# A gated recurrence and a mixture of experts in fp32: the recurrence on two sequences at a time, with matmuls that alternate between halves of the array

## The chip, the cores and the metric

One core of a Trainium2 chip. The metric is the device time of one execution in microseconds: 672.98 us for the kernel before, the median of three runs (672.84 to 673.34).

## The reference

Two parts in a row, all in fp32. The first is a recurrence per batch b and head h (4 x 8 of them, 768 steps, head size 48) whose state, a 48x48 matrix, decays by a gate f per row and step:

```python
f = 1.0 / (1.0 + np.exp(-f_logit))
for t in range(S):
    state = f[:, :, t, :, None] * state + np.einsum('bhd,bhe->bhde', k[:, :, t], v[:, :, t])
    y[:, :, t] = np.einsum('bhd,bhde->bhe', q[:, :, t], state)
```

Its 3072 x 384 output x goes into the second part: each token takes the best of 4 groups (logits `x @ w_group`), in it the best of 4 experts (`x @ w_expert[g]`), and gets `gate * relu(x @ w1) @ w2` of that one expert (w1 384x1024, w2 1024x384).

## The kernel before, in words

**The recurrence** (L111 to L248) works on chunks of 128 tokens of one sequence, `order` = chunk by chunk and within it sequence by sequence, 24 chunks in all. A chunk goes through five stages, functions of the kernel, and in step i of a loop the five stages run on five chunks, the oldest first:

- `gated` (L131): loads f, q, k and v (192 KB each, SP queue); exp and ln on ScalarE (ACT) make -log f; a matmul with `cum` (tile cs) sums it from the chunk's middle; transposes (nt) and a reduction give the chunk's whole decay; exp of the sums, times q and k, gives qh (VectorE, DVE) and kh (GpSimd, POOL).
- `turned` (L166): transposes qh and kh, so that heads lie on partitions, two heads a on the two halves of 64 (rows 0 to 47 and 64 to 111): tiles Tq and Tk.
- `scored` (L176): ap = k q^T for each head (48 rows of the array, 128 columns), first the four heads of the lower half of partitions, then those of the upper; DVE masks it with `tri` into am.
- `weighed` (L187): y = am v (128 rows, 48 columns) and sp q (48 rows, 48 columns; sp is the scaled state), first one half, then the other; ACT copies y to xT. ds = kh v updates the state st.
- `done` (L219): gate logits lg = gw xT (20 x 128, stationary gw) into logitsT, transposes back to tokens (x_ps), DVE copies x, SP stores it to x_dram.

A matmul in fp32 is two passes on TensorE (PE) in the trace, each with its own weight load; a transpose is one. Tiles of PSUM come from one pool of 8 banks in rotation. Tile, the scheduling layer, puts each engine's instructions in an order of its own, and the engine follows that in order.

**The join**: when all chunks are done, a flag `fari` (the largest sum of -log f against a bound) is read by every engine, and a branch skips the slow exact scan. **The routing** (L317 to L437) starts with 24 transposes of logitsT (tile logits, L343) and is a chain on DVE after that. **The experts** (L440 on): 16 experts, 256 slots each, weights three deep in the pool `wp`; the weights of the first experts are loaded in the recurrence already.

Of the kernel before, what the change touches and what calls it, by code (L numbers as in the profile page):

```python
# [1 line left out]

# [6 lines left out]
FP32 = mybir.dt.float32  # L9
# [6 lines left out]
P = 128  # L16
# [3 lines left out]
def kernel(  # L20
# [38 lines left out]
    wp = ctx.enter_context(tc.tile_pool(name="wp", bufs=3))  # L59
# [14 lines left out]
    tri = const([P, P], FP32, "tri")            # 1 where row <= column  # L74
    strict = const([P, P], FP32, "strict")      # 1 where row < column
    cum = const([P, P], FP32, "cum")            # sums from the chunk's middle
# [10 lines left out]
    nc.vector.tensor_scalar(cum, tri, halves[:, 0:1], None, OP.subtract)  # L87
# [5 lines left out]
    # gate weights with the rows in the order of xT: a head to each 64 partitions  # L93
    gw = const([P, HP, NL], FP32, "gw")
    nc.vector.memset(gw, 0.0)
    for r in range(2):
        rows = slice(DP * r, DP * r + D)
        nc.sync.dma_start(out=gw[rows, :, 0:G], in_=moe_w_group.rearrange("(a r d) g -> r d a g", r=2, d=D)[r])
        for g in range(G):
            nc.sync.dma_start(out=gw[rows, :, G + g * EG:G + (g + 1) * EG], in_=moe_w_expert[g].rearrange("(a r d) e -> r d a e", r=2, d=D)[r])  # L100

    logitsT = const([NL, N], FP32, "logitsT")
    sums = const([P, NT, HP, 2], FP32, "sums")

    def chunk_logits(n, xT):
        lg = bank([NL, P], "lg")
        for a in range(HP):
            nc.tensor.matmul(lg, lhsT=gw[:, a, :], rhs=xT[:, a, :], start=(a == 0), stop=(a == HP - 1))  # L108
        nc.vector.tensor_copy(logitsT[:, n * P:(n + 1) * P], lg)  # L109

# [1 line left out]
    with ExitStack() as fast:  # L112
        sb = fast.enter_context(tc.tile_pool(name="sb", bufs=3))
        NROT = 5
        pads = {}
        for nm in ("nl", "qh", "kh"):
            pads[nm] = [const([P, H, DP], FP32, f"{nm}{i}") for i in range(NROT)]
            for t in pads[nm]:
                nc.vector.memset(t[:, :, D:DP], 0.0)
        NX = 3  # L120
        xTs = [const([P, HP, P], FP32, f"xT{i}") for i in range(NX)]
        for t in xTs:
            nc.vector.memset(t, 0.0)
        state = {}

        order = [(b, c) for c in range(NC) for b in range(B)]
        live = {}

        def gated(i):
            """Loads, decay sums, and the gated q and k with heads on partitions."""  # L130
            b, c = order[i]  # L131
            n = b * NC + c
            ld = {}
            for nm, src in (("f", f_logit), ("q", q), ("k", k), ("v", v)):
                ld[nm] = sb.tile([P, H, D], FP32, tag="ld_" + nm, bufs=5, name="ld_" + nm)
                nc.sync.dma_start(out=ld[nm], in_=src[b, :, c * P:(c + 1) * P, :].rearrange("h t d -> t h d"))
            nl, qh, kh = (pads[nm][i % NROT] for nm in ("nl", "qh", "kh"))

            # -log f = ln(1 + exp(-f_logit)); a value below -44 is over SAFE and sets the scan going
            ex = sb.tile([P, H, D], FP32, tag="ex", name="ex")  # L140
            nc.vector.tensor_scalar(ex, ld["f"], -44.0, None, OP.max)
            nc.scalar.activation(ex, ex, AF.Exp, bias=0.0, scale=-1.0)
            nc.scalar.activation(nl[:, :, 0:D], ex, AF.Ln, bias=1.0, scale=1.0)  # L143

            cs = bank([P, DM], "cs")
            nc.tensor.matmul(cs.rearrange("t (h d) -> t h d", d=D), lhsT=cum, rhs=nl[:, :, 0:D], start=True, stop=True)  # L146
            nt = bank([P, HP, P], "nt")
            nlp = nl.rearrange("t (a r) d -> t a (r d)", r=2)
            for a in range(HP):
                nc.tensor.transpose(out=nt[:, a, :], in_=nlp[:, a, :], identity=ident)  # L150
            # the bounds are met by every sum below SAFE; they keep what the scan replaces finite
            mid = sb.tile([P, DM], FP32, tag="mid", name="mid")
            nc.vector.tensor_scalar(mid, cs, SAFE, -SAFE, OP.min, OP.max)
            nc.vector.reduce_sum(out=sums[:, n], in_=nt.rearrange("p a (e t) -> p a e t", e=2), axis=AX)
            gl = sb.tile([P, HP, 2], FP32, tag="gl", bufs=4, name="gl")
            nc.scalar.activation(gl, sums[:, n], AF.Exp, bias=0.0, scale=-1.0)
            eq = sb.tile([P, DM], FP32, tag="eq", name="eq")
            ek = sb.tile([P, DM], FP32, tag="ek", name="ek")
            nc.scalar.activation(ek, mid, AF.Exp, bias=0.0, scale=1.0)  # L159
            nc.scalar.activation(eq, mid, AF.Exp, bias=0.0, scale=-1.0)  # L160
            nc.gpsimd.tensor_tensor(kh[:, :, 0:D], ld["k"], ek.rearrange("t (h d) -> t h d", d=D), OP.mult)  # L161
            nc.vector.tensor_tensor(qh[:, :, 0:D], ld["q"], eq.rearrange("t (h d) -> t h d", d=D), OP.mult)
            live[i] = {"v": ld["v"], "qh": qh, "kh": kh, "gl": gl}

        def turned(i):
            w = live[i]  # L166
            for nm in ("q", "k"):
                pt = bank([P, HP, P], "tr_" + nm)
                tp = w[nm + "h"].rearrange("t (a r) d -> t a (r d)", r=2)
                for a in range(HP):  # L170
                    nc.tensor.transpose(out=pt[:, a, :], in_=tp[:, a, :], identity=ident)
                w[nm] = sb.tile([P, HP, P], FP32, tag="T" + nm, name="T" + nm)
                (nc.vector.tensor_copy if nm == "q" else nc.scalar.copy)(w[nm], pt)

        def scored(i):
            w = live[i]  # L176
            w["am"] = []
            for r in range(2):
                rows = slice(DP * r, DP * r + D)
                ap = bank([P, HP, P], "ap")  # L180
                for a in range(HP):
                    nc.tensor.matmul(ap[:, a, :], lhsT=w["k"][rows, a, :], rhs=w["q"][rows, a, :], start=True, stop=True)  # L182
                t = sb.tile([P, HP, P], FP32, tag=f"am{r}", bufs=2, name=f"am{r}")
                nc.vector.tensor_tensor(t, ap, tri.unsqueeze(1).broadcast_to((P, HP, P)), OP.mult)  # L184
                w["am"].append(t)

        def weighed(i):  # L187
            """The chunk's outputs, and the state that it leaves."""
            b, c = order[i]
            w = live[i]  # L190
            gl = w["gl"]
            if c:
                sp = sb.tile([P, HP, D], FP32, tag="sp", name="sp")
                nc.vector.tensor_tensor(sp, state[b], gl[:, :, 0:1].broadcast_to((P, HP, D)), OP.mult)
            w["xT"] = xT = xTs[i % NX]
            for r in range(2):
                rows = slice(DP * r, DP * r + D)
                y = bank([P, HP, P], "y")
                for a in range(HP):
                    nc.tensor.matmul(y[rows, a, :], lhsT=w["v"][:, 2 * a + r, :], rhs=w["am"][r][:, a, :], start=(a == 0), stop=(c == 0), skip_group_check=True)  # L200
                if c:
                    for a in range(HP):
                        nc.tensor.matmul(y[rows, a, :], lhsT=sp[rows, a, :], rhs=w["q"][rows, a, :], start=False, stop=True, skip_group_check=True)  # L203
                nc.scalar.copy(xT[rows], y[rows])  # L204

            if c < NC - 1:
                ds = bank([P, HP, D], "ds")
                for a in range(HP):
                    for r in range(2):
                        nc.tensor.matmul(ds[DP * r:DP * r + DP, a, :], lhsT=w["kh"][:, 2 * a + r, :], rhs=w["v"][:, 2 * a + r, :], start=True, stop=True)  # L210
# [317 lines left out]
```

## Time and profile before

| what | before |
|---|---|
| median of the runs | 672.98 us |
| the profiled execution: span of its instructions | 672.1 us |
| of this: recurrence, to the last x_ps on PE | 0 to 246.0 us |
| flag, branch, routing, to the first expert matmul | 246.0 to 298.8 us |
| experts | 298.8 to 672.1 us |
| PE busy | 604.9 us (90%) |
| DVE, ACT, POOL busy | 240.6, 116.0, 89.8 us |

The profiled execution is known by its span; the runs' median is 0.9 us above that, for what lies around the span. A timeline row has the start, the duration of the whole group, engine, line, operation, tiles, and shapes; "48*128 48x128" is 48 rows and 128 columns of the array with 48x128 moving elements. PE is pipelined, so a pass is longer (some 0.27 us) than the step from one pass to the next: time per stage is read from the start of one group to the start of the next. The granted clock printed for the first 28 us is not to be trusted; durations tell it there.

### The profile page before, as it was taken

The numbers are of one execution on the slowest core, as the hardware profiler recorded it, in microseconds if no ns is written. First come the engines' busy times: TensorE is split into PE (matmuls) and PEld (weight loads), VectorE is DVE, ScalarE is ACT, GpSimd is POOL, SyncE is SP. The second block draws the span as 40 slices with busy tenths as digits, with TensorE's granted clock in tenths as the row PEclk, the third lists the DMA queues.
The fourth block names the chain that finished last, engine by engine and source line by source line (L and its number), as shares of the span: only waits on it lengthen the run. The fifth ranks groups of instructions, "written<-read, shape, count | busy, mean of one in ns | idle before, by whom it ended". The sixth has DMA issues, their size and how long they took to land. (4 is left out here: it accounts for less than half of the span.)

```text
span 672.1 us, 8713 instructions
## 1 busy us (share of the span) xinstructions
PE 604.9 (90%) x3485; PEld 461.8 (69%) x3485; DVE 240.6 (36%) x548; ACT 116.0 (17%) x258; POOL 89.8 (13%) x104
## 2 busy tenths in 40 slices
PE   4999999999999963569999999999999999999993
PEld 2788888888888842447766776677667767776772
DVE  4586557556555426931111111111111211121110
ACT  3454444333322210000000000000000000000000
POOL 1111011011001000040121122012201220111001
PEclk9999999999999996559999999999999999999998
DMA  6577666858660000023463646264635453540000
GB/s 122 115 150 158 130 131 142 212 155 241 152 205 27 24 27 1 0 81 108 135 228 109 213 138 223 109 217 140 207 127 203 149 195 139 185 140 17 13 7 19
DMA packets 132562, 85.62 MB, mean 127 GB/s; under 512 B 104208, under 2 KB 123701, under 8 KB 132514
## 3 DMA queue, kind: packets, MB, share of 16 engines
q1 hardware_dynamic: 128418, 73.97, 38.7%
q0 software_dynamic: 4096, 11.02, 4.6%
q8 instruction: 30, 0.49, 0.3%
q14 instruction: 18, 0.15, 0.1%
HBM read 75.53 MB, written 11.01 MB: 129 GB/s over the span
## 5 line engine op out<-in xcount | busy, mean ns | idle before, releaser
L461 PE MATMUL hp<-xe,w 128*128 128x256 f32 x768 | 173.1, 386 | 15.4 <-DVE xe L456 15.4
L461 PEld LDWEIGHTS hp<-xe,w 128*128 128x128 f32 x768 | 146.7, 193 | 39.3 <-DVE xe L456 19.4
L469 PE MATMUL yo<-w,h 128*128 128x384 f32 x512 | 167.7, 486 | 0.0
L469 PEld LDWEIGHTS yo<-w,h 128*128 128x128 f32 x512 | 97.3, 190 | 64.4
L465 ACT ACTIVATE h<-hp 128x256 f32<-128x256 f32 x64 | 24.5, 383 | 368.3 <-PE hp L461 324.0
L463 DVE TENSOR_SCALAR h<-hp 128x256 f32<-128x256 f32 x64 | 27.2, 424 | 154.2 <-PE hp L461 112.0
L471 DVE TENSOR_SCALAR yt<-yo,slots 128x384 f32<-128x384 f32 x32 | 19.8, 618 | 148.5 <-PE yo L469 148.5
L472 POOL DMA_INDIRECT out_dram<-yt,slot_tok x32 | 32.3, 1010 | 256.1 <-DVE yt L471 248.3
L161 POOL TENSOR_TENSOR kh<-ld_k,ek 128x384 f32<-128x384 f32 x24 | 24.1, 1003 | 198.2 <-ACT ek L159 129.7
L200 PE MATMUL y<-am,ld_v 128*48 128x128 f32 x384 | 50.5, 283 | 0.0
L200 PEld LDWEIGHTS y<-am,ld_v 128*48 128x48 f32 x384 | 39.0, 126 | 8.0 <-DVE logitsT L109 3.9
L444 POOL DMA_INDIRECT xg<-x_dram,slot_tok x32 | 31.2, 974 | 90.8 <-PE xg_ps L455 45.7
L203 PE MATMUL y<-Tq,sp 48*48 48x128 f32 x320 | 42.8, 274 | 0.0
L182 PE MATMUL ap<-Tq,Tk 48*128 48x128 f32 x384 | 42.4, 291 | 0.0
L182 PEld LDWEIGHTS ap<-Tq,Tk 48*128 48x128 f32 x384 | 37.7, 193 | 2.0 <-issue 0.6
L204 ACT COPY xT<-y 48x512 f32<-48x512 f32 x48 | 27.7, 577 | 64.7 <-PE y L203 61.2
L184 DVE TENSOR_TENSOR am<-ap,tri 128x512 f32<-128x512 f32 x48 | 31.2, 686 | 20.7 <-PE ap L182 20.7
L203 PEld LDWEIGHTS y<-Tq,sp 48*48 48x48 f32 x320 | 32.6, 119 | 7.4 <-issue 7.4
L146 PE MATMUL cs<-nl,cum 128*128 128x384 f32 x48 | 22.0, 542 | 9.6 <-ACT nl L143 9.6
L428 PE MATMUL table<-val,lane 128*128 128x108 f32 x48 | 15.3, 486 | 11.7 <-DVE val L427 11.7
L108 PE MATMUL lg<-xT,gw 128*20 128x128 f32 x192 | 25.2, 274 | 0.7 <-ACT xT L204 0.7
L428 PEld LDWEIGHTS table<-val,lane 128*128 128x128 f32 x48 | 12.1, 313 | 15.9 <-DVE val L427 12.9
(123 smaller groups left out, 453.7 us busy)
## 6 DMA issues: line engine op xcount, KB each, us to landing
w<-in_moe_w_dram SPq DMA_DIRECT2D x32, 1536.0 KB, 7.2
ld_f<-in_f_logit_dram SPq DMA_DIRECT2D x24, 192.0 KB, 3.7
ld_q<-in_q_dram SPq DMA_DIRECT2D x24, 192.0 KB, 3.7
ld_k<-in_k_dram SPq DMA_DIRECT2D x24, 192.0 KB, 3.7
ld_v<-in_v_dram SPq DMA_DIRECT2D x24, 192.0 KB, 3.0
x_dram<-x SPq DMA_DIRECT2D x24, 192.0 KB, 2.0
xg<-x_dram,slot_tok POOLq DMA_INDIRECT x32, 5.1
out_dram<-yt,slot_tok POOLq DMA_INDIRECT x32, 2.6
```

The source lines that it names most:

```text
L108: nc.tensor.matmul(lg, lhsT=gw[:, a, :], rhs=xT[:, a, :], start=(a == 0), stop=(a == HP - 1))
L182: nc.tensor.matmul(ap[:, a, :], lhsT=w["k"][rows, a, :], rhs=w["q"][rows, a, :], start=True, stop=True)
L184: nc.vector.tensor_tensor(t, ap, tri.unsqueeze(1).broadcast_to((P, HP, P)), OP.mult)
L200: nc.tensor.matmul(y[rows, a, :], lhsT=w["v"][:, 2 * a + r, :], rhs=w["am"][r][:, a, :], start=(a == 0), stop=(c == 0), skip_group_check=True)
L203: nc.tensor.matmul(y[rows, a, :], lhsT=sp[rows, a, :], rhs=w["q"][rows, a, :], start=False, stop=True, skip_group_check=True)
L204: nc.scalar.copy(xT[rows], y[rows])
L428: nc.tensor.matmul(table.rearrange("p b t -> p (b t)"), lhsT=lane, rhs=val.rearrange("p b t -> p (b t)"), start=(n == 0), stop=(n == NT - 1))
L444: nc.gpsimd.indirect_dma_start(out=t, out_offset=None, in_=x_dram[:, :], in_offset=bass.IndirectOffsetOnAxis(ap=rows, axis=0))
L461: nc.tensor.matmul(hp, lhsT=w1[:, ko, fo * P:(fo + 1) * P], rhs=xt[:, ko, :], start=(ko == 0), stop=(ko == KO - 1))
L463: nc.vector.tensor_scalar(h[:, fo, :], hp, 0.0, None, OP.max)
L469: nc.tensor.matmul(yp, lhsT=h[:, fo, j * P:(j + 1) * P], rhs=w2[:, fo, :], start=(fo == 0), stop=(fo == FO - 1))
L472: nc.gpsimd.indirect_dma_start(out=out, out_offset=bass.IndirectOffsetOnAxis(ap=rows[j], axis=0), in_=y, in_offset=None, bounds_check=N - ...
```

## The change

The unit of work is now one chunk of two sequences (12 units, pairs s of sequences), and the loop has 16 steps in place of 28. What is computed of the reference is the same.

- All tiles of `gated` have a dimension for the two sequences: 384 KB loads, 768 elements per partition for ACT, DVE and POOL. The sums run from the chunk's start (`tri` in place of `cum`), so the clamp `mid`, the reduction `sums` and the transposes nt are gone; the chunk's whole decay g is the last column of transposes of eq (gt). eq is made by ACT straight from PSUM. qh moves from DVE to POOL, kh from POOL to DVE, the copy Tq from DVE to ACT.
- `scored` alternates lower and upper half of the rows matmul by matmul, into two banks. `weighed` puts the two sequences on the two halves of the columns: y from the state uses all four quarters in turn, y from am the two column halves. `done` has the two sequences on two row halves, and the logits' matmul is turned round: xT is the stationary side (48 rows x 128 columns), gw the moving one (20 columns), so logits come out with tokens on partitions (lgall) and the routing's 24 transposes go.
- The stages are generators, cut where a bank is finished, and a table (WEAVE) sets how they are interleaved in one step.
- The loads of gw move from the SP queue to the ACT queue. Recurrence pools have two buffers; the third pair of expert weights has a pool of its own (wq), which takes the room that the recurrence leaves, so it is loaded after the branch.

The core of the diff:

```diff
-        order = [(b, c) for c in range(NC) for b in range(B)]
+        units = [(c, s) for c in range(NC) for s in range(B // 2)]
...
+    lgall = const([P, NT, NL], FP32, "lgall")
...
-        nc.sync.dma_start(out=gw[rows, :, 0:G], in_=moe_w_group.rearrange("(a r d) g -> r d a g", r=2, d=D)[r])
+        nc.scalar.dma_start(out=gw[rows, :, 0:G], in_=moe_w_group.rearrange("(h d) g -> d h g", d=D))
...
+            for b in range(2):
+                cs = bank([P, H, D], "cs")
+                nc.tensor.matmul(cs.rearrange("t h d -> t (h d)"), lhsT=tri, rhs=nl[:, b], start=True, stop=True)
+                nc.scalar.activation(eq[:, b, :, 0:D], cs, AF.Exp, bias=0.0, scale=-1.0)
+                nc.scalar.activation(ek[:, b], cs, AF.Exp, bias=0.0, scale=1.0)
+                yield
+            nc.gpsimd.tensor_tensor(heads(qh)[:, :, 0:D], heads(w["q"]), heads(eq)[:, :, 0:D], OP.mult)
+
+            nc.vector.scalar_tensor_tensor(out=heads(kh)[:, :, 0:D], in0=heads(ek), scalar=math.exp(SAFE), in1=heads(w["k"]), op0=OP.min, op1=OP.mult)
...
         def scored(i):
             w = live[i]
...
-            for r in range(2):
-                rows = slice(DP * r, DP * r + D)
-                ap = bank([P, HP, P], "ap")
-                for a in range(HP):
-                    nc.tensor.matmul(ap[:, a, :], lhsT=w["k"][rows, a, :], rhs=w["q"][rows, a, :], start=True, stop=True)
+            for b in range(2):
+                ap = [bank([P, HP, P], f"ap{r}") for r in range(2)]
                 for a in range(HP):
                     for r in range(2):
+                        rows = slice(DP * r, DP * r + D)
+                        nc.tensor.matmul(ap[r][:, a, :], lhsT=w["Tk"][rows, b, a, :], rhs=w["Tq"][rows, b, a, :], start=True, stop=True)
+                for r in range(2):
+                    nc.vector.tensor_tensor(w["am"][:, b, r], ap[r], tri.unsqueeze(1).broadcast_to((P, HP, P)), OP.mult)
+                yield
...
+            if c:
+                for a in range(HP):
+                    for r in range(2):
+                        rows = slice(DP * r, DP * r + D)
+                        for b in range(2):
+                            nc.tensor.matmul(ys[r][DP * b:DP * b + DP, a, :], lhsT=old[rows, b, a, :], rhs=w["Tq"][rows, b, a, :], start=(a == 0), stop=False, skip_group_check=True)
+            yield
+            for a in range(HP):
+                for r in range(2):
+                    for b in range(2):
+                        nc.tensor.matmul(ys[r][DP * b:DP * b + DP, a, :], lhsT=w["v"][:, b, 2 * a + r, :], rhs=w["am"][:, b, r, a, :], start=(c == 0 and a == 0), stop=True, skip_group_check=True)
...
+            lg = [bank([P, NL], f"lg{b}") for b in range(2)]
+            for h in range(H):
+                for b in range(2):
+                    rows = slice(DP * b, DP * b + D)
+                    nc.tensor.matmul(lg[b], lhsT=xT[rows, h % 2, h // 2, :], rhs=gw[rows, h, :], start=(h == 0), stop=(h == H - 1))
...
+        WEAVE = (("s", 1), ("t", 1), ("d", 1), ("s", 1), ("t", 1), ("d", 1), ("g", 1), ("w", 2), ("t", 1), ("w", 1), ("g", 1), ("t", 1), ("g", 1), ("d", 1), ("t", 1), ("g", 1))
...
-        logits = bank([P, NT, NL], "logits")
-        for n in range(NT):
-            nc.tensor.transpose(out=logits[:, n, :], in_=logitsT[:, n * P:(n + 1) * P], identity=ident[0:NL, 0:NL])
-        L = logits.rearrange("p n (a e) -> p n a e", e=4)
+        L = lgall.rearrange("p n (a e) -> p n a e", e=4)
```

How the instructions stand. On PE, before, one step of the loop in the middle of the recurrence (each row's last number is how often it repeats):

```order
L200 MATMUL y<-am_1546,ld_v 48x128 x4
L203 MATMUL y<-Tq,sp 48x128 x4
L200 MATMUL y<-am_1553,ld_v 48x128 x4
L203 MATMUL y<-Tq,sp 48x128 x4
L210 MATMUL ds<-ld_v,kh_134 64x48 x8
L182 MATMUL ap<-Tq,Tk 128x128 x8
L171 MATMUL tr_q<-ident,qh_121 128x128 x4
L171 MATMUL tr_k<-ident,kh_131 128x128 x4
L146 MATMUL cs<-nl_112,cum 128x384
L150 MATMUL nt<-ident,nl_112 128x128 x4
L108 MATMUL lg<-xT_142,gw 20x128 x4
L227 MATMUL x_ps<-ident,xT_142 128x128 x4
```

Each stage is one piece, and each half of the array has its piece.

On PE, after, from the end of the second scores to the state's part of y; ap_1155 is the bank of the lower half, ap_1156 that of the upper:

```order
L189 MATMUL ap_1155<-Tq,Tk 128x128
L189 MATMUL ap_1156<-Tq,Tk 128x128
L169 MATMUL tr_k<-ident,kh_133 128x128 x4
L239 MATMUL x_ps_1173<-ident,xT 128x128 x4
L205 MATMUL y_1191<-Tq,st_0_140 64x128 x2
L205 MATMUL y_1192<-Tq,st_0_140 64x128 x2
```

The scores now change halves with every matmul; transposes of two other stages stand between them and y, and y has two column halves (x2) per row half.

On PE, after, the rest of that step:

```order
L210 MATMUL y_1191<-am,v_112 64x128 x2
L210 MATMUL y_1192<-am,v_112 64x128 x2
L169 MATMUL tr_q<-ident,qh_127 128x128 x4
L220 MATMUL ds<-v_112,kh_131 64x48 x16
L152 MATMUL cs<-ex,tri 128x384
L169 MATMUL tr_k<-ident,kh_133 128x128 x4
L152 MATMUL cs<-ex,tri 128x384
L246 MATMUL lg_1268<-gw,xT 128x20
L246 MATMUL lg_1269<-gw,xT 128x20
```

After the last lg come eight transposes gt, and the next step begins with ap. The exp and ln that cs waits for stand on ACT behind the first copy Tq of the same step.

## Rows read from the trace of the kernel before

**Rows 1.** The page: the engines' busy time, and PE's granted clock in 40 slices.
```profile
PE 604.9 (90%) x3485; PEld 461.8 (69%) x3485; DVE 240.6 (36%) x548; ACT 116.0 (17%) x258; POOL 89.8 (13%) x104
PEclk9999999999999996559999999999999999999998
```

**Rows 2.** Two windows: busy us and instructions per engine, clock, DMA share, GB/s.
```profile
10.00:20.00 10.00, 7.49 (x30) 5.62 (x30) 3.98 (x9) 2.92 (x8) 2.02 (x2) 1.00 1.03 202
60.00:100.00 40.00, 40.00 (x371) 32.68 (x372) 25.20 (x51) 17.18 (x37) 4.02 (x4) 1.00 0.64 134
```

**Rows 3.** Timeline of PE for one chunk's step; start us, duration us of the group.
```profile
159.84 1.71 PE L182 MATMUL ap<-Tq,Tk 48*128 48x128 f32 x16
161.48 0.66 PE L171 MATMUL tr_q<-ident,qh 128*128 128x128 f32 x4
161.97 0.60 PE L171 MATMUL tr_k<-ident,kh 128*128 128x128 f32 x4
162.41 0.81 PE L146 MATMUL cs<-nl,cum 128*128 128x384 f32 x2
163.06 0.60 PE L150 MATMUL nt<-ident,nl 128*128 128x128 f32 x4
163.59 1.05 PE L108 MATMUL lg<-xT,gw 128*20 128x128 f32 x8
164.57 0.66 PE L227 MATMUL x_ps<-ident,xT 128*128 128x128 f32 x4
165.15 1.07 PE L200 MATMUL y<-am,ld_v 128*48 128x128 f32 x8
166.16 1.07 PE L203 MATMUL y<-Tq,sp 48*48 48x128 f32 x8
...
169.16 0.67 PE L210 MATMUL ds<-ld_v,kh 128*64 128x48 f32 x16
169.77 0.37 PE L182 MATMUL ap<-Tq,Tk 48*128 48x128 f32 x1
```

**Rows 4.** Windows of L210 (ds) alone: passes on PE and PEld begun so far.
```profile
159.20:159.24 0.04, 0.00 (x1) 0.00 (x1) 1.00 0.75 307
159.20:159.25 0.05, 0.01 (x2) 0.01 (x2) 1.00 0.99 410
```

**Rows 5.** The same of L200 (y), where a sequence's first chunk has no state.
```profile
48.70:49.18 0.48, 0.47 (x4) 0.47 (x5) 1.00 0.97 199
48.70:49.20 0.50, 0.49 (x6) 0.49 (x7) 1.00 0.98 200
48.70:49.62 0.92, 0.91 (x12) 0.91 (x13) 1.00 0.99 201
```

**Rows 6.** The same of L182 (ap), where the lower half gives way to the upper.
```profile
159.80:160.60 0.80, 0.76 (x7) 0.76 (x9) 1.00 0.63 241
159.80:160.62 0.82, 0.78 (x9) 0.78 (x11) 1.00 0.62 235
```

**Rows 7.** Groups of instructions on DVE, ACT and POOL: busy us, mean ns of one, idle.
```profile
L184 DVE TENSOR_TENSOR am<-ap,tri 128x512 f32<-128x512 f32 x48 | 31.2, 686 | 20.7 <-PE ap L182 20.7
L204 ACT COPY xT<-y 48x512 f32<-48x512 f32 x48 | 27.7, 577 | 64.7 <-PE y L203 61.2 <-PE y L200 3.4
L161 POOL TENSOR_TENSOR kh<-ld_k,ek 128x384 f32<-128x384 f32 x24 | 24.1, 1003 | 198.2 <-ACT ek L159 129.7 <-PE lg L108 44.6 <-DMA ld_q<-in_q_dram 8.7
L162 DVE TENSOR_TENSOR qh<-ld_q,eq 128x384 f32<-128x384 f32 x24 | 19.5, 814 | 0.0
L159 ACT ACTIVATE ek<-mid 128x384 f32<-128x384 f32 x24 | 12.4, 517 | 14.3 <-DVE mid L153 14.3
```

**Rows 8.** Timeline at the recurrence's start, on PE: the pipeline fills.
```profile
6.83 1.65 PE L146 MATMUL cs<-nl,cum 128*128 128x384 f32 x2 [6.83 <-ACT nl L143]
8.27 1.06 PE L150 MATMUL nt<-ident,nl 128*128 128x128 f32 x4
...
28.89 1.71 PE L182 MATMUL ap<-Tq,Tk 48*128 48x128 f32 x16
```

**Rows 9.** Timeline at its end: last transposes, then the first work behind the branch.
```profile
245.35 0.66 PE L227 MATMUL x_ps<-ident,xT 128*128 128x128 f32 x4
...
252.30 2.71 PE L343 MATMUL logits<-ident,logitsT 20*128 20x20 f32 x24 [6.18 <-DVEq L261]
...
255.05 0.66 DVE L346 TENSOR_REDUCE mx<-logits 128x120 f32<-128x480 f32 x1 [1.83 <-PE logits L343]
```

More of the change, by code (lines that the diff above doesn't have):

```diff
@@ L118 @@
             for t in pads[nm]:
[L119 to L124, printed above, removed]
-        order = [(b, c) for c in range(NC) for b in range(B)]
+                nc.gpsimd.memset(t[:, :, :, D:DP], fill)
+        states = [[kept([P, 2, HP, DP], f"st{s}_{i}") for i in range(2)] for s in range(B // 2)]
+        for pair in states:
+            for t in pair:
+                nc.gpsimd.memset(t[:, :, :, D:DP], 0.0)
@@ L127, with heads @@
+        units = [(c, s) for c in range(NC) for s in range(B // 2)]
+        NU = len(units)
         live = {}
+        def heads(t):
+            return t.rearrange("p b h d -> p (b h) d")
         def gated(i):
[L131 to L136, printed above, removed]
@@ L163, in gated @@
-            live[i] = {"v": ld["v"], "qh": qh, "kh": kh, "gl": gl}
+            c, s = units[i]
+            w = live[i] = {}
+            for nm, src in (("f", f_logit), ("k", k), ("q", q), ("v", v)):
+                if nm == "v":
+                    w[nm] = pads["v"][i % 5]
+                else:
+                    w[nm] = sb.tile([P, 2, H, D], FP32, tag="ld_" + nm, name="ld_" + nm)
+                nc.sync.dma_start(out=heads(w[nm])[:, :, 0:D], in_=src[2 * s:2 * s + 2, :, c * P:(c + 1) * P, :].rearrange("b h t d -> t (b h) d"))
@@ L187, in weighed @@
[L187 to L207, printed above, removed]
+            w["am"] = sb.tile([P, 2, 2, HP, P], FP32, tag="am", name="am")
@@ L220, in done @@
+            yield
         def done(i):
[L221 to L230 removed]
@@ L232 @@
-        stages = (gated, turned, scored, weighed, done)
-        for i in range(NT + len(stages) - 1):
-            for late in reversed(range(len(stages))):
-                if 0 <= i - late < NT:
-                    stages[late](i - late)
+            c, s = units[i]
+            xT = live[i]["xT"]
+            x = sb.tile([P, 2, HP, 2, D], FP32, tag="x", name="x")
+            for r in range(2):
+                pt = bank([P, HP, 2, DP], f"x_ps{r}")
+                for a in range(HP):
+                    nc.tensor.transpose(out=pt[:, a].rearrange("t b d -> t (b d)"), in_=xT[:, r, a, :], identity=ident)
+                nc.vector.tensor_copy(x[:, :, :, r, :], pt[:, :, :, 0:D].rearrange("t a b d -> t b a d"))
+                yield
@@ L301 @@
             nc.sync.dma_start(out=y_dram[bass.ds(i, 1)].rearrange("o (c p) w -> (o p) c w", p=P), in_=ys)
+        gwp = sb.tile([P, HP, NL], FP32, tag="gwp", bufs=1, name="gwp")
+        for r in range(2):
+            rows = slice(DP * r, DP * r + DP)
+            nc.vector.tensor_copy(gwp[rows], gw.rearrange("p (a r) l -> p a r l", r=2)[rows, :, r, :])
         for n in range(NT):
@@ L313 @@
             nc.scalar.copy(xT, pt)
-            chunk_logits(n, xT)
+            lg = bank([P, NL], "lg")
+            for a in range(HP):
+                nc.tensor.matmul(lg, lhsT=xT[:, a, :], rhs=gwp[:, a, :], start=(a == 0), stop=(a == HP - 1))
+            nc.vector.tensor_copy(lgall[:, n, :], lg)
     gate = const([P, NT], FP32, "gate")
```

151 lines of the change are left out of this document (79 added, 72 removed).

## The prediction

> **What bounds the kernel now.** The page comes first: PE is busy 90% of the span, the next engine 36% [rows 1]. A window of four chunks' steps says it sharper: PE 40.00 of 40.00 us, ACT and DVE near half, DMA 0.64 [rows 2]. So in the recurrence a pass saved on PE is time saved, as long as nothing else comes last. The experts behind it are not touched; only the recurrence and its join to the routing count.
>
> The timeline of one step gives the price list [rows 3]. From start to start: ap 1.64 us, four transposes 0.44 (161.97 to 162.41), cs 0.65, lg 0.98, each half of y 1.00 (165.15 to 166.16), ds 0.61; the step 9.93 (159.84 to 169.77). Eight passes of y take 1.00, four transposes in a row 0.44: a pass of 128 columns is 0.11 us, and a change of the array's shape (rows, columns, or all) costs some 0.13 more. I price all blocks with these two.
>
> **Do halves run side by side in fp32?** That is the whole question, and before answers for pairs, since at a few places halves already meet. ds alternates column halves: one pass has begun at 159.24, two at 159.25 [rows 4], and its 16 passes take 0.61. In the first chunk of a sequence no state stands between the halves of y: there two passes begin within 49.18 and 49.20, and from 49.20 to 49.62 six more, a pass per 0.07 where one half alone goes at 0.11 (the sixth pass of the stream opens the second half) [rows 5]. In ap, two passes begin within 160.60 and 160.62, at the place where the lower rows give way to the upper [rows 6]. So column halves overlap, row halves overlap, also with loads of 128 columns (ap). Four quarters at once occur nowhere.
>
> **The sum, per unit of two chunks.** Before: 2 x 9.93 = 19.9 us. After, by the order of the step, with p = 0.11 and 0.13 for a change:
>
> - ap: 2 x (8 slots, each a pair: 0.88 + 0.13) = 2.0; before 3.3.
> - tr_q and tr_k with x_ps: 2 x (8 p + 0.13) = 2.0; tr_q of the other sequence 0.6.
> - y from the state: 32 passes. Four at a time 8 slots, 1.0; two at a time 1.9; one by one 3.6 (before 4.0). I take 1.0, since pairs of both kinds overlap; 1.9 is the other end.
> - y from am: 32 passes in pairs, 16 p + 0.13 = 1.9; before 4.0.
> - ds: alternates already, 1.1.
> - cs, tr_k, cs: 0.65 + 0.44 + 0.65 + 0.13 = 1.9.
> - lg: 32 passes in pairs. They stream 20 columns but load 128. Nearest row: ap's pairs with 128-column loads, so 16 p + 0.13 = 1.9, about what 2 x 0.98 was; if loads cost nothing, 16 x 20/128 x 0.11 + 0.13 = 0.4.
> - gt: 1.0; in place of nt, 2 x 0.53.
>
> Together 13.4, with lg's and ap's changes a bit dearer 13.5: 6.4 us less per unit.
>
> **Do the others keep up?** From the groups [rows 7], at 13.5 us per unit. ACT: exp, ln, two eq, two ek, 6 x 384 elements of ek's kind or twice as long, some 3.9, six copies of 512 (0.58) 3.5, two small: 7.8. DVE: four am 2.7, kh of 768 elements 1.6 (twice the mean 0.81 of qh, which had POOL beside it), and, at am's rate of 0.69 per 512 elements, two x, sp and st of 384 2.1 and ex of 768 1.0: 7.4. POOL: qh twice 1.0 = 2.0. DMA: 1.97 MB per unit; at 202 GB/s, where it was full (share 1.03) [rows 2], 9.7 us; with the 6.3 MB of two experts' weights 148 us over the recurrence, less than what follows for PE. So none bounds by its sum, but two chains are close. qh: from the last cs over eq (0.52) and POOL (2.0) and their waits, some 3.2, to the next tr_q, against lg, gt and ap on PE, 3.9. am: from the end of the second ap two masks and an x copy, 1.9 to 2.1, against tr_k, x_ps and y from the state, 2.0. I cost them at nothing in the middle of the forecast, and 1 us per step is the upper bound I give them.
>
> **Fill.** Before, PE first works at 6.83, cs takes 1.44 (6.83 to 8.27) where it takes 0.65 later [rows 3, 8], so the clock is at its lower level although the page prints 9 there [rows 1]; the fifth step begins at 28.89. After, the four first steps do twice the data along the same chain (load, ex, exp, ln, cs, eq, qh, transposes, copies), and ten gw loads stand ahead of exp on ACT; the next step's exp stands behind the copies on ACT, so the chains add. Bounds: 40 if most of it overlaps, 57.8 if everything doubles. I walk it with doubled element counts: qh at 15, the second step's qh at 27, the third's at 40, the fifth step at 50. I take 50.
>
> **Steps 5 to 16.** The first has no state (12.5), seven are full (94.5), then the stages fall away: 12.2 without cs, 8.2 without cs, transposes and ds, 5.9 with y, x_ps and lg, 2.9 with x_ps and lg. Sum 136.2; 2.3 for waits in the tail. End of the recurrence: 50 + 136.2 + 2.3 = 188.5, against 246.0 before [rows 9]: 57.5 less.
>
> **Join.** The branch takes the same (246.0 to 252.3). Behind it, mx waited for 24 transposes, 252.30 to 255.05 [rows 9]; it now starts at once: 2.4 less. The third expert's weights come after the branch, with some 50 us of routing and two experts as cover: nothing. If that cover went, its 3 MB would be 15 us at 202 GB/s, and the third expert would wait.
>
> Sum: -57.5 - 2.4 = -59.9. The profiled span was 672.1, the median 672.98; the difference carries over unchanged: **613 us**.
>
> **Rivals.**
> 1. *PE waits for its neighbours.* The two close chains, or the eight banks (19 per step now, 11 per chunk before), stretch the step to 15.5 to 17 us. For it: margins of 0.1 to 0.7 us, POOL and DVE slowing each other (qh's 384 elements on DVE take 0.81 in the mean, am's 512 only 0.69). Against: idle is half of each engine. Over nine steps 18 to 32 us: 631 to 645. Of this the Trainium skill speaks (TensorEngine Tiling (Array Packing), PSUM Bottleneck): tiling speeds up TensorE but not the emptying of PSUM, which may become the bottleneck. No trace before shows it; the first run will.
> 2. *Quarters go two at a time.* No row shows four. 0.9 us x 10 units with a state: 622.
> 3. *The clock falls to its lower level in the middle, slower than before.* At that level passes take twice as long (cs 1.44 against 0.65). Place: each step now has 2 us of lg with 20 columns and 5 us of transposes, streaming less. At the lower level throughout, the steps 5 to 16 take 272 in place of 136: 749. It decides from where the step exceeds 19.9, that is if it spends over 0.47 of its full-speed time so. Against: the clock was granted in full from the fill to the end of the recurrence [rows 1], through lg and transposes in every step. The Trainium skill (TensorE: Matmul & The Clock Gate, Part 4) states that the full clock does not engage for transposes, which do not count as busy alike; here they ran at 0.11 per 128 columns like y [rows 3], so the trace differs from it in the mixed stream.
>
> That halves take turns altogether, so that the change does nothing of what it says, is excluded by rows 4 to 6; what is left of it is rival 2.
>
> **Chances.** Forecast 0.70, rival 1 0.17, rival 2 0.08, rival 3 0.05. Time 613. The forecast's own spread is 600 (fill of 42, cheap lg in part) to 630 (fill of 57, 0.8 us of waits per step); with rival 2 and the near half of rival 1 the range is 600 to 638, which leaves out rival 3, the far half of rival 1 and the tails, under 2 in 10. Faster by over 0.2% (about what a measurement of this kernel can tell from no change): 0.70 + 0.17 + 0.08 = 0.95; of rival 3, 0.01 lies at the break-even and 0.04 beyond.
>
> **What would show it.** A full step on PE of 13 to 14 us, without idle; ap, y and lg with passes that begin in pairs, y from the state 32 passes in 1.0 us; clock in full from 30 to 195 us; last x_ps or lg near 188; mx within 0.5 us behind the branch. Idle on PE before tr_q or y, named for POOL's qh or DVE's am, would be rival 1; y from the state at 1.9 rival 2; a step that begins long after 50 would make my fill wrong; experts that start late for the third expert's weights, the join.

## The result, and the profile after

The changed kernel takes **611.52 us** (median of 4 runs, 608.70 to 613.11), the kernel before 672.91 us beside it (4 runs, 672.46 to 673.34): a ratio of **0.908**, interval 0.905 to 0.910. Forecast were 613 us, and a range of 600 to 638. The profiled execution took 610.75 us with a span of 609.0, against a span of 672.1 before.

The page after, the lines that answer to [rows 1]:

```profile
PE 533.1 (88%) x3653; PEld 405.8 (67%) x3653; DVE 178.6 (29%) x394; ACT 106.9 (18%) x234; POOL 91.8 (15%) x109
PEclk9989999999995656999999999999999999999997
```

PE's busy time fell by 71.8 us, though it runs 168 passes more. A window of full steps, columns as in [rows 2]:

```profile
60.00:100.00 40.00, 40.00 (x579) 33.43 (x577) 21.02 (x35) 21.57 (x44) 4.90 (x4) 1.00 0.88 186
```

PE still has no idle at all, at the full clock, now with 1.56 times as many passes per window (579 against 371); DVE and ACT are again near half. So PE still sets the pace of the recurrence, and what it saves is time. One step, the PE timeline; it answers to [rows 3], but for two chunks in place of one:

```profile
133.20 1.10 PE L205 MATMUL y<-Tq,st 48*64 48x128 f32 x32
134.24 1.97 PE L210 MATMUL y<-am,v 128*64 128x128 f32 x32
136.13 0.66 PE L169 MATMUL tr_q<-ident,qh 128*128 128x128 f32 x4
136.72 1.14 PE L220 MATMUL ds<-v,kh 128*64 128x48 f32 x32
137.79 0.91 PE L152 MATMUL cs<-ex,tri 128*128 128x384 f32 x2
...
139.72 1.97 PE L246 MATMUL lg<-gw,xT 48*128 48x20 f32 x32
141.61 1.09 PE L177 MATMUL gt<-ident,eq 128*128 128x128 f32 x8
142.63 1.16 PE L189 MATMUL ap<-Tq,Tk 48*128 48x128 f32 x16
143.73 0.66 PE L169 MATMUL tr_q<-ident,qh 128*128 128x128 f32 x4
...
146.86 1.10 PE L205 MATMUL y<-Tq,st 48*64 48x128 f32 x32
```

From y to y it is 13.66 us, 6.83 a chunk where it was 9.93. From start to start, 32 passes of y from the state take 1.04 us: a pass every 0.033, while one pass alone steps at 0.11. Windows of this block alone, columns as in [rows 4], show that four passes begin within 0.03 us, and the next four within 0.20:

```profile
133.20:133.23 0.03, 0.03 (x4) 0.03 (x4) 1.00 1.45 237
133.20:133.40 0.20, 0.20 (x8) 0.20 (x12) 1.00 1.34 219
```

So all four quarters of the array are at work at once.

The start, on ACT and on PE (two views). The first exp waits for the loads of gw that stand ahead of it in ACT's queue; the fifth step's first ap is the last row:

```profile
8.59 0.84 ACT L144 ACTIVATE ex<-ex 128x768 f32<-128x768 f32 x1 [6.58 <-DMA gw<-in_moe_w_group_dram]
```

```profile
27.18 0.66 PE L169 MATMUL tr_q<-ident,qh 128*128 128x128 f32 x4 [0.17 <-POOL qh L156]
...
38.55 0.66 PE L169 MATMUL tr_q<-ident,qh 128*128 128x128 f32 x4 [0.56 <-POOL qh L156]
...
47.17 1.16 PE L189 MATMUL ap<-Tq,Tk 48*128 48x128 f32 x16
```

The end, on PE and on DVE, against [rows 9]: the small transpose behind the last lg, and hp, the first expert's first matmuls (x w1); then, on POOL and on DVE, the first work behind the branch.

```profile
185.57 0.28 PE L267 MATMUL wt<-ident,worst 128*1 128x128 f32 x1
...
237.04 12.23 PE L492 MATMUL hp<-xe,w 128*128 128x256 f32 x48 [0.65 <-DVE xe L487]
```

```profile
191.36 0.14 POOL L364 IOTA first<- 128x4 f32 x1 [35.20 <-PEq L288]
...
193.21 0.65 DVE L377 TENSOR_REDUCE mx<-lgall 128x120 f32<-128x480 f32 x1 [6.69 <-issue]
```

The recurrence ends at 185.85 (185.57 + 0.28) in place of 246.0: 60.15 us less. From there to mx it is 7.36 us in place of 9.05: 1.7 less. From mx to the first hp 43.83 in place of 43.74. From hp's start to the end of the span 1.4 us less, as the first hp takes 12.23 where it took 13.65 (start 298.79): the clock rose 3.3 us behind its start in this execution, 6.1 in the other. Together 60.15 + 1.7 - 0.1 + 1.4 = 63.15, the difference of the two spans. The medians differ by 61.4.

### The profile page after: what moved, and what is told of

It is laid out like the page before. It is cut to its first block, busy times and chain, and to the rows that moved or that the text cites. A ratio compares the mean times of both kernels' runs of the same rounds, so it can differ in the third digit from the quotient of the medians.

```text
span 609.0 us, 8706 instructions
## 1 busy us (share of the span) xinstructions
PE 533.1 (88%) x3653; PEld 405.8 (67%) x3653; DVE 178.6 (29%) x394; ACT 106.9 (18%) x234; POOL 91.8 (15%) x109
## 5 line engine op out<-in xcount | busy, mean ns | idle before, releaser
L156 POOL TENSOR_TENSOR qh<-ld_q,eq 128x768 f32<-128x768 f32 x12 | 22.2, 1854 | 128.0 <-ACT eq L153 106.5
L152 PE MATMUL cs<-ex,tri 128*128 128x384 f32 x48 | 24.3, 597 | 15.4 <-ACT ex L145 15.4
L158 DVE SCALAR_TENSOR_TENSOR kh<-ek,ld_k 128x768 f32<-128x768 f32 x12 | 21.3, 1775 | 25.2 <-ACT ek L154 25.2
L189 PE MATMUL ap<-Tq,Tk 48*128 48x128 f32 x384 | 27.9, 285 | 0.0
L189 PEld LDWEIGHTS ap<-Tq,Tk 48*128 48x128 f32 x384 | 23.3, 187 | 4.0 <-issue 3.4
L246 PEld LDWEIGHTS lg<-gw,xT 48*128 48x128 f32 x384 | 22.4, 188 | 5.0 <-issue 4.9
L210 PE MATMUL y<-am,v 128*64 128x128 f32 x384 | 23.6, 276 | 0.0
L246 PE MATMUL lg<-gw,xT 48*128 48x20 f32 x384 | 23.6, 264 | 0.0
L210 PEld LDWEIGHTS y<-am,v 128*64 128x64 f32 x384 | 20.7, 137 | 2.1 <-issue 2.1
L152 PEld LDWEIGHTS cs<-ex,tri 128*128 128x128 f32 x48 | 8.7, 223 | 17.1 <-issue 11.0
```

What stands on the lines that cost most here:

```text
L152: nc.tensor.matmul(cs.rearrange("t h d -> t (h d)"), lhsT=tri, rhs=nl[:, b], start=True, stop=True)
L189: nc.tensor.matmul(ap[r][:, a, :], lhsT=w["Tk"][rows, b, a, :], rhs=w["Tq"][rows, b, a, :], start=True, stop=True)
L210: nc.tensor.matmul(ys[r][DP * b:DP * b + DP, a, :], lhsT=w["v"][:, b, 2 * a + r, :], rhs=w["am"][:, b, r, a, :], start=(c == 0 and a == 0) ...
L246: nc.tensor.matmul(lg[b], lhsT=xT[rows, h % 2, h // 2, :], rhs=gw[rows, h, :], start=(h == 0), stop=(h == H - 1))
```

## The experiments

Times are medians, ratios against the kernel before; the changed kernel is 611.52 us, 0.908. In the diffs "-" is the changed kernel unless said otherwise. Where a time at which the clock fell or rose is given, it is from the trace's clock records.

### Halves in turn

**All four pairings undone.** The same passes, one half or quarter to its end before the next; ds stays as it is.

```diff
-                for a in range(HP):
-                    for r in range(2):
+                for r in range(2):
+                    for a in range(HP):
...
-            for h in range(H):
-                for b in range(2):
+            for b in range(2):
+                for h in range(H):
```

(ap and lg are shown; y from the state and from am likewise.)

> Only the order of the matmuls is changed: ap, y from the state, y from am and lg do one half (quarter) to its end before the next begins; ds stays. Theory (the halves' overlap on TensorE is the whole gain): per step ap goes from 2 x 1.09 to 2 x 1.64 us as before, y from the state from 1.04 to 2.6 to 3.6, y from am and lg from 1.89 to 3.3 to 3.6 each; the step from 13.66 to 19 to 21 us, the time to 670 to 690 us. Rival (the gain comes from larger and fewer instructions on the other engines, or from the weave): under 625 us.

Measured 739.13 us, 1.098 (1.093 to 1.102): slower than before the change. PE's timeline through one step that runs at the full clock up to its end:

```profile
87.13 3.33 PE L246 MATMUL lg<-gw,xT 48*128 48x20 f32 x32
...
91.41 1.71 PE L189 MATMUL ap<-Tq,Tk 48*128 48x128 f32 x16
93.05 0.66 PE L169 MATMUL tr_q<-ident,qh 128*128 128x128 f32 x4
...
96.74 2.56 PE L205 MATMUL y<-Tq,st 48*64 48x128 f32 x32
99.23 3.33 PE L210 MATMUL y<-am,v 128*64 128x128 f32 x32
102.49 0.66 PE L169 MATMUL tr_q<-ident,qh 128*128 128x128 f32 x4
...
106.07 3.33 PE L246 MATMUL lg<-gw,xT 48*128 48x20 f32 x32
109.33 1.59 PE L177 MATMUL gt<-ident,eq 128*128 128x128 f32 x8
110.85 3.09 PE L189 MATMUL ap<-Tq,Tk 48*128 48x128 f32 x16
```

The step is 18.94 us (87.13 to 106.07), at the lower end of what was expected, and block by block the pairing's worth is read: ap 1.64 against 1.09, y from the state 2.49 against 1.04, y from am 3.26 against 1.89, lg 3.26 against 1.89. Over all steps, with the first and last ones, that is 12 x (1.1 + 1.37 + 1.37) + 10 x 1.45 = 61 us, for 672, about the time of the kernel before. The rest was not foreseen, and the page shows it:

```profile
PEclk9997795675976565555599999999999999999998
```

The clock fell again and again in the recurrence, first at 65.4 and 109.8 us; the second fall is the step above, right behind lg, where gt takes 1.52 us (109.33 to 110.85) in place of 1.02 and ap 3.02 (110.85 to 113.87) in place of 1.64. In the recurrence 158 us passed at the lower level. If half of that is lost, it is 672 + 79 = 751, where the profiled run took 742.8: the sum is 8 us too high, and where those are is not shown.

**Only lg in turn** (the second pair of the diff above), and **all but lg in turn**.

> Only lg goes in turn, all else as the changed kernel. Theory (lg in turn lets the clock fall): the block goes from 1.89 to 3.26 us, and the granted clock falls behind it in many steps, 640 to 680 us. Rival (lg costs its passes alone): 611.5 + 12 x 1.37 = 628 us at full clock.

656.26 us, 0.975 (0.968 to 0.982). The step at the full clock is 15.02 us, 1.36 more. PE's timeline, then the windows before and behind the clock's fall (columns as above, the clock third from the end):

```profile
94.42 3.33 PE L246 MATMUL lg<-gw,xT 48*128 48x20 f32 x32
...
109.44 3.32 PE L246 MATMUL lg<-gw,xT 48*128 48x20 f32 x32
112.70 1.52 PE L177 MATMUL gt<-ident,eq 128*128 128x128 f32 x8
```

```profile
109.40:113.20 3.80, 3.80 (x38) 3.73 (x38) 0.57 (x3) 1.25 (x3) 1.82 (x1) 1.00 0.43 87
113.20:120.00 6.80, 6.80 (x46) 5.75 (x44) 2.97 (x5) 2.52 (x5) 0.00 (x0) 0.50 0.86 166
```

lg ends at 112.70, and at 113.2 the clock falls to half, with PE busy throughout. In the recurrence 70 us passed at the lower level: 12 x 1.36 + 35 = 51 us, for 663; the profiled run took 660.6.

> As the run with all halves in turn, but lg alternates again; that run had a granted clock at the lower level in stretches that begin at or just behind lg (65.4, 109.8, 137.1, 167.8 us). Theory (lg in turn, 3.3 us of 20 columns behind loads of 128, is what lets the clock fall; the rest of the loss is the overlap alone): clock in full through the steps, a step of 13.66 + 2 x 0.55 (ap) + 1.45 (y from the state) + 1.37 (y from am) = 17.6 us, 611.5 + 13 + 14.5 + 16.5 = 655 us. Rival (y in single quarters and halves lets it fall): lower level in most steps, over 690 us.

Its two runs lie 18 us apart (661.03 and 679.30, mean clock 0.940 and 0.912), so no interval is given. The profiled one is the longer. Its step at the full clock is 17.58 us (lg from 97.42 to 115.00), as expected; the clock fell three times for 17 us, the first at 118.2, 1.3 us behind the end of lg:

```profile
115.00 1.97 PE L246 MATMUL lg<-gw,xT 48*128 48x20 f32 x32
116.90 1.09 PE L177 MATMUL gt<-ident,eq 128*128 128x128 f32 x8
117.92 2.82 PE L189 MATMUL ap<-Tq,Tk 48*128 48x128 f32 x16
```

12 x 2.47 + 10 x 1.45 = 44, and half of 51 is 26: 681 for a run of 679.3. The shorter run, 661.03, is 5.5 us above 611.5 + 44; it has no profile, so what its clock did is not known. So the blocks' prices are borne out, and without lg in turn the lower level took 51 us in place of 158. In the profiled run the clock fell even so, each time behind lg; why it fell there, with lg paired again, is open.

### Two quarters in place of four

Of y from the state alone, upper rows after lower; the two column halves still alternate.

```diff
-                for a in range(HP):
-                    for r in range(2):
+                for r in range(2):
+                    for a in range(HP):
                         for b in range(2):
```

> Only y from the state: the outer loop is the row half, so the column halves alternate within it, two at a time, and four quarters never follow each other. Theory (four quarters run at once): that block goes from 1.04 to 1.9 us, 0.85 us over ten units with a state, 8 to 9 us more, near 620 us. Rival (quarters only ever ran in pairs, or something else bounds the step): block and time unchanged, 611 to 612 us.

617.29 us, 0.918 (0.915 to 0.920), 5.8 more than with four.

```profile
106.98 1.59 PE L205 MATMUL y<-Tq,st 48*64 48x128 f32 x32
108.50 1.97 PE L210 MATMUL y<-am,v 128*64 128x128 f32 x32
```

The block takes 1.52 us, between the 1.04 of four in turn and the 2.49 of one quarter after the other. That is 0.48 x 10 = 4.8 of the 5.8 us. Four quarters do overlap. Two at a time were cheaper than the 1.9 that the prediction gave them, because the upper pair starts before the lower one is through, as ap did in [rows 6]: in the trace 10 passes begin in the first 0.5 us of the block, 14 in the next 0.4, and 8 in the rest.

### The order within a step

**No weave**: each stage as a whole.

```diff
-        WEAVE = (("s", 1), ("t", 1), ("d", 1), ("s", 1), ("t", 1), ("d", 1), ("g", 1), ("w", 2), ...
+        WEAVE = (("d", 3), ("w", 3), ("s", 2), ("t", 5), ("g", 4))
```

> Only the table that weaves the stages: each stage is one piece again, the oldest unit first. Theory (TensorE sets the step, and the stage order only decides how often the array changes shape): TensorE stays without idle in the full steps and changes shape about five times less per step at 0.13 us, so the step falls from 13.66 to 13.0 to 13.2 us, 603 to 608 us. Rival (the weave is what hides the chains of qh and am and the rotation of banks): TensorE waits, the step is over 15 us and the time over 625 us.

602.88 us, 0.897 (0.894 to 0.899): 8.6 us faster than the change. PE has no idle here either, and the step is 12.67 us:

```profile
112.14 1.10 PE L205 MATMUL y<-Tq,st 48*64 48x128 f32 x32
...
124.81 1.10 PE L205 MATMUL y<-Tq,st 48*64 48x128 f32 x32
```

The woven step changes the array's shape 11 times, this one 5 times: (13.66 - 12.67) / 6 = 0.165 us a change in the mean. The Trainium skill (TensorEngine Tiling (Array Packing), Key Properties) says that a change of tiling mode drains TensorE; the runs agree and give this price. The recurrence ends 9.7 us sooner (176.1 in place of 185.85), but the full steps are the smaller part of it: seven of them are 7.0 us less, and two falls of the clock for 3.4 us (at 72.0 and 99.3), which the woven one had not, take back 3.3. The fifth step begins 3.5 us sooner (43.68 in place of 47.17) and is itself 1.9 shorter, and the tail gives 0.7. Behind the recurrence 1.4 us are lost again, half of them in the first hp (12.94 in place of 12.23).

**No weave, the gate's loads later, lg between ds and ap**; and the same with the next unit's loads, exp and ln issued ahead, qh and kh per sequence.

```diff
+        WEAVE = (("d", 2), ("w", 3), ("d", 1), ("s", 2), ("t", 5), ("g", 4))
...
+            if i == 1:
+                load_gate()
```

```diff
+                nc.gpsimd.tensor_tensor(qh[:, b, :, 0:D], w["q"][:, b], eq[:, b, :, 0:D], OP.mult)
+                nc.vector.scalar_tensor_tensor(out=kh[:, b, :, 0:D], in0=ek[:, b], ...
...
+            if i + 1 < NU:
+                readied(i + 1)
```

> Stages in one piece each as in the run without the weave, gw loaded late, and lg moved between ds and ap, with whose shape it agrees. Theory (TensorE sets the step by its passes and changes of shape; lg behind transposes caused the two short falls of the clock, 3.4 us each, of the run without the weave): step 12.66 to 12.5 us, no fall, fifth step 2 us earlier: 602.9 - 2 - 1.7 - 3 = 596 us, 594 to 600. Rival (neither matters): 601 to 604 us.

597.80 us, 0.887 (0.885 to 0.889): 5.1 less than without the weave alone. The step at the full clock is 12.56 us, 0.11 less for one change of shape less; but in the profiled run the clock fell three times for 3.4 us, where the theory had no fall.

> As the one before, and qh and kh are made for one sequence at a time as soon as its eq and ek are there, and the loads, exp and ln of the next unit are issued at the end of a step. Theory (the fill is a chain through qh, the copies, exp, ln and cs): the fifth step begins 4 to 7 us sooner, the full steps stay, 590 to 593 us. Rival (in the fill TensorE's lower clock level sets the pace, or more instructions on POOL and DVE lengthen the full steps): within 2 us of the one before.

595.12 us, 0.884 (0.881 to 0.886): 2.7 less, as the first x_ps of the fifth step begins at 38.41 in place of 41.46, which is less than the 4 to 7 us of the theory. Its clock falls three times too. One of the falls in windows (clock third from the end), with the stretch before it, and the lg ahead of it:

```profile
95.00:98.70 3.70, 3.70 (x82) 3.65 (x80) 1.88 (x6) 1.35 (x3) 0.00 (x0) 1.00 0.72 186
98.70:102.10 3.40, 3.40 (x26) 3.18 (x23) 2.58 (x4) 0.57 (x1) 0.00 (x0) 0.50 1.02 207
```

```profile
95.82 1.96 PE L252 MATMUL lg<-gw,xT 48*128 48x20 f32 x32
97.63 2.82 PE L195 MATMUL ap<-Tq,Tk 48*128 48x128 f32 x32
```

**lg cut in two.** Against the last one; the halves stand before y and behind ds.

```diff
             for h in range(H):
...
+                if h == H // 2 - 1:
+                    yield
...
-        WEAVE = (("d", 2), ("w", 3), ("d", 1), ("s", 2), ("t", 5), ("g", 4))
+        WEAVE = (("d", 3), ("w", 3), ("d", 1), ("s", 2), ("t", 5), ("g", 4))
```

> e8_fill with lg cut in two: the first four heads' 16 passes before y, the other 16 behind ds, where all 32 stood. In e8 the granted clock fell three times in the recurrence (57.7, 85.0 and 98.7 us), each time within 1.4 us behind the end of lg or in the block behind it. Theory: lg's short columns in one piece, with the transposes near it, let the clock fall; cut in two it holds. Then no fall or one in the middle, the step 12.6 + 0.1 us, 591 to 593 us. Rival: what counts is how the whole step is mixed, wherever lg stands: two or three falls again, 595 to 597 us.

**590.93 us**, 0.878 (0.877 to 0.879), the fastest of all, and its five runs lie within 1.1 us where the last kernel's lie within 3.5. No fall in the recurrence from 29.6 to 166.1 us, as the clock's line of its page shows (each digit 14.7 us); the step is 12.67:

```profile
PEclk9899999999965559999999999999999999999997
```

```profile
64.44 1.10 PE L211 MATMUL y<-Tq,st 48*64 48x128 f32 x32
...
68.29 1.07 PE L252 MATMUL lg<-gw,xT 48*128 48x20 f32 x16
69.20 2.04 PE L195 MATMUL ap<-Tq,Tk 48*128 48x128 f32 x32
...
77.11 1.10 PE L211 MATMUL y<-Tq,st 48*64 48x128 f32 x32
```

Some 0.1 us more per step, 1.3 us in all, against three falls that cost half of 10.2: -3.8, measured -4.2. The two ran on different chips; a run with the last kernel's recurrence on this one's chip (594.91, below) stands 4.0 above it too, with one fall in its profile. So with the same transposes and the same passes in both, it is the cut of lg and its new places that go with a clock that holds; which of the two it is, was not tried apart.

**The same cut in the changed kernel**, woven as it is. This takes lg from between the last cs and ap.

```diff
-        WEAVE = (... ("d", 1), ("g", 1), ("w", 2), ("t", 1), ("w", 1), ("g", 1), ("t", 1), ("g", 1), ("d", 1), ("t", 1), ("g", 1))
+        WEAVE = (... ("d", 2), ("g", 1), ("w", 2), ("t", 1), ("w", 1), ("d", 1), ("g", 1), ("t", 1), ("g", 1), ("t", 1), ("g", 1))
```

> The changed kernel as it is, with lg cut in two as in e9: heads 0 to 3 between the last x_ps and y from the state, the others behind ds. The number of shape changes in a step stays the same. The changed kernel's runs lay between 608.7 and 613.1 us, those of e9 within 1.1 us. Theory: part of that spread is falls of the clock behind lg, which only other runs than the profiled one had; cut in two, runs within 1.5 us of each other, step 13.6 to 13.8 us, median 608 to 610 us. Rival: the woven step already holds the clock, and the spread comes from behind the recurrence, where the clock rises at a different time in each run: spread of 4 us again, 610 to 612 us.

616.93 us, 0.917 (0.915 to 0.918): 5.4 slower, and neither theory had it. The step is 14.50 us (ap at 116.20, then 130.70), with a wait that the changed kernel doesn't have in a full step:

```profile
129.73 1.04 PE L177 MATMUL gt<-ident,eq 128*128 128x128 f32 x8
130.70 1.16 PE L189 MATMUL ap<-Tq,Tk 48*128 48x128 f32 x16
132.66 0.66 PE L169 MATMUL tr_q<-ident,qh 128*128 128x128 f32 x4 [0.80 <-POOL qh L156]
```

Nine such waits from 45 to 190 us, 7.2 us in all. That is rival 1 after all, in the place that the prediction named as close: from the end of cs over eq and POOL's qh to tr_q it takes 2.93 us (129.73 to 132.66). In the changed kernel lg, gt and ap cover that with 4.01 (139.72 to 143.73); without lg 2.1 are left. The clock held in both, so of the spread of the changed kernel's runs (4.4 us; here 2.5) this tells little.

### The gate's loads, and the experts' first matmuls

**Loads of gw behind the second unit's loads, on SP.**

```diff
-        nc.scalar.dma_start(out=gw[rows, :, 0:G], ...
+            nc.sync.dma_start(out=gw[rows, :, 0:G], ...
```

> Only the ten loads of gw: they leave the ACT queue and stand on the SP queue behind the loads of the second unit. Theory (the fill is one chain through ACT): the first exp starts at 6.3 to 6.6 us in place of 8.59, and the fifth step, which began at 47.17, begins 1.5 to 2.2 us sooner, the time falls by as much, to 609 to 610 us. Rival (the fill is set by something behind it, as the granted clock or the loads): the fifth step begins at 46.7 to 47.5, time unchanged.

610.78 us, 0.908 (0.906 to 0.910). The first exp starts at 6.37 instead of 8.59 and the fifth step at 45.09 instead of 47.17, as expected, but the median moves by 0.7, less than the runs differ among themselves. The loads cost the fill 2.1 us; that they cost the kernel as much is not shown.

**Filler for PE before the first expert.** Matmuls that nobody reads, ahead of the first hp: seven against the kernel of 595.12, then six against that of 590.93.

```diff
+        for _ in range(6):
+            warm = bank([2 * NB, DM], "warm")
+            nc.tensor.matmul(warm, lhsT=slots.rearrange("p b t -> p (b t)"), rhs=..., start=True, stop=True)
```

> e8_fill with seven matmuls of 384 columns, whose results nobody reads, behind the 48 of the slot table, where PE then waits 4.8 us for the gathered rows. Theory: the experts' first hp (13.02 us in e8, 10.63 for the second expert) starts at the lower clock because PE idled before it; worked for 3 to 4.5 us more just before, it gets the full clock sooner: first hp 10.6 to 11.5, 592.5 to 594 us. Rival: the waits of 0.5 to 0.7 us behind it or the lower clock of the filler itself undo it: hp 12 to 13 again, or the gathered rows' transposes begin later, 595 to 596 us.

594.91 us, 0.886 (0.883 to 0.888): no change. The scheduler put the seven among the slot table's matmuls, and the first hp took 12.70 us.

> e9_split_lg with six matmuls of 384 columns that take the finished slot table as their weights, so that they can't start before it; nobody reads what they give. In e10 the filler ran among the table's own matmuls and the clock was low again at the first hp (12.70 us). Theory: 4 us of work in the wait of 4.8 us just before the gathered rows bring the full clock sooner: first hp 10.6 to 11.5 in place of 12.82, 588.5 to 590 us. Rival: the two waits of 0.5 and 0.65 us behind it keep the clock low until hp itself has run: hp 12.5 to 13 again, 590.5 to 591.5 us.

597.79 us, 0.888 (0.886 to 0.890): 6.9 slower. PE's and POOL's timelines:

```profile
210.31 6.92 PE L473 MATMUL warm<-ohe,slots 128*108 128x384 f32 x12 [0.36 <-DVE slots L469]
...
224.58 13.11 PE L504 MATMUL hp<-xe,w 128*128 128x256 f32 x48 [0.65 <-DVE xe L499]
```

```profile
218.22 1.15 POOL L487 DMA_INDIRECT xg<-x_dram,slot_tok  x1 [43.55 <-PE warm L473]
```

The filler took 6.92 us in place of 4 (12 passes, most of them at the lower clock), the gather of the tokens waited for its end (it began at 209.98 without the filler), and the first hp was no faster. The theory has fallen: the clock rose at 216.0 for 3.4 us and was low again before hp.

## Why the prediction was right

**What bounds the kernel** was read right: PE, before and after, without idle in a full step.

**The step** was forecast at 13.4 to 13.5 us and is 13.66. By its terms, forecast and measured: ap 2.0 and 2.2; tr_q and tr_k with x_ps 2.0 and 2.0; the other tr_q 0.6 and 0.6; y from the state 1.0 and 1.04; y from am 1.9 and 1.89; ds 1.1 and 1.07; cs, tr_k, cs 1.9 and 1.93; lg 1.9 and 1.89; gt 1.0 and 1.02. Two numbers from [rows 3], a pass of 0.11 us and a change of shape of 0.13, priced nine blocks to 0.2 us. What was missing stands in ap: 1.09 to 1.10 a block for 1.01. The 0.165 a change of the run without the weave would give 0.4 more over the 11 changes, which is more than was missing; it is a mean, and what single changes cost is not measured.

**That halves overlap in fp32** was read from three places in the trace of before [rows 4 to 6], and that four quarters do was inferred, without a row for it: right, 1.04 us. With rival 2 the block would have taken 1.52, not 1.9.

**lg** was the term with the widest bounds (0.4 to 1.9), taken by ap's row with the same loads: right. In turn it takes 3.26 us for 32 passes of 20 columns, the same as y from am with 128. A fixed price of every pass it isn't, since the 32 passes of ds, 48 columns behind loads of 64, take 1.07 where lg's, paired alike, take 1.89. So the load of 128 columns is likely what sets its price; no run changes the load alone. Turning it round gained nothing on lg itself (0.98 a chunk before, 0.95 now); it took the 24 transposes off the join. The Trainium skill (TensorEngine Tiling (Array Packing), Instruction Overhead) warns that a matmul with one moving column takes as long as one with 60. Here it is harsher: 20 take as long as 128, where each has a load of 128 columns of its own.

**The others keep up**: ACT was forecast at 7.8 us per unit and shows 7.4 (21.57 of 40 us, times 13.66), DVE at 7.4 and shows 7.2. Rival 1 did not come: one wait of 0.8 us for qh in the whole recurrence behind the fill. What the Trainium skill holds possible there, that emptying PSUM becomes the bottleneck, did not come in this kernel: PE has no wait in a full step, and both engines that empty PSUM are idle half of the time. But the margin of the qh chain was as thin as written: 2.93 us of chain (forecast 3.2) under 4.01 of cover (3.9), and the woven cut lost 7.2 us by taking lg out of that cover.

**Rival 3**, the clock, did not come in the profiled run: full from 35.5 us, not from 30, to the end of the recurrence. The other three runs have a lower mean clock (0.936 to 0.944, here 0.950) and no profile, so where theirs was lower is not known. What spoke for the rival was right all the same: lg, with its 20 columns, was the place. With lg in turn the clock falls within it or right behind it, and the lower level then takes about twice as long, as priced. The transposes that the Trainium skill names there do not do it alone: the run with lg cut in two has them all and holds the clock.

**The fill** was walked to 50 and ended at 47.17. The second qh was forecast for 27 and the third for 40; tr_q began at 27.18 and 38.55. So the error of 2.8 us came in the last two steps. From there to the end the forecast was 136.2 + 2.3 = 138.5, measured 138.7 (47.17 to 185.85). That this fits so well is luck: the 2.3 us stood for waits in the tail, and PE has no wait there. They paid for the seven full steps, dearer by 0.16 each, and for the fifth step, dearer by 1.0, most of it the one wait for qh.

**The join** failed by 0.7 us: mx did not start "at once". Behind the branch POOL starts at 191.36, DVE only at 193.21, so 1.7 us were saved and not 2.4; flag and branch took 0.8 less (5.5 from the end of the recurrence to POOL's start, 6.3 before). What DVE waits for the profile doesn't show. And 1.4 us came where nothing was forecast, from an earlier rise of the clock in the first expert, which is luck of the two executions. The sum: -60.15 for -57.5, -1.7 for -2.4, -1.3 for 0, together -63.15 for -59.9.

**From span to median** the prediction carried 0.9 us over unchanged, and that was wrong. In every run with a span on record the time is 1.75 to 1.9 us above the span, so the profiled execution of before was some 1.0 us slower than the median beside it, while that of after was 0.8 faster. That takes 1.75 off the 63.15, and with it the median comes to 1.5 us from the forecast, closer than the terms are.

## What to carry to other kernels

Where PE bounds and half of the array stands empty, look in the old trace for places where halves already meet by chance: they price the pairing before it is written, and order alone (alternate, not in turn) makes it. Price a step by two numbers, the pass and the change of shape, and then count the changes: here each one that the weave added cost 0.165 us in the mean, and its full steps hid nothing by it. And try where a block like lg stands, and know which chain it covers: the same 32 passes of lg cost the clock in one place, a wait of 0.8 us per step in another, and nothing in a third.

## What was not expected of the hardware

- **The clock falls with PE busy, and at lg.** In the trace of before it fell only when PE went idle [rows 1], at 250.3 and 267.4 us and behind the last matmuls. Seven of the profiles of other orders show 30 falls inside the recurrence, behind its fill, and all 30 lie among the passes of lg or at most 2.1 us behind the start of its last one (falls at or behind the last lg of all, where the recurrence ends, are not counted), though lg is 1.8 to 3.3 us of a step of 12.6 to 19. In the unwoven step with lg whole it fell one to three times for 3.4 us (four profiles); with lg cut in two, in neither of two. The woven step held it with lg whole (three profiles) and cut (one). What in the mix decides is open.
- **Order buys twice.** Undoing the pairing cost 61 us by its passes and about 70 more by the clock.
- **The gather waited for the filler**, though it uses nothing of what the filler gives. The filler reads `ohe`, a tile of the routing's pool, and the gathered rows go into a pool that opens when that one has closed; that they take over its room, and so wait for its last reader, is possible and was not tried.
